# Attention stage of a fused attention, expert and feed-forward kernel: scatters, ranks and GpSimd's weight chunks get other steps

## The chip, the cores and the metric

The program runs on one core of one Trainium2 chip. The metric is the device time of one execution in microseconds; the kernel before and the changed kernel are timed in several runs each and compared by their medians. The engines are named as in the profile: PE is TensorE's matrix multiplication and PEld its weight load, DVE is VectorE, ACT is ScalarE, POOL is GpSimd and SP is SyncE, which here only issues transfers.

## The reference, cut to what matters

The inputs q and k are scaled by constant factors before the call. Three stages follow each other: attention with a window of 128, a mixture of 8 experts with the best two experts per token, and a feed-forward layer. Only the middle of the first two stages is touched by the change.

```python
# attention: batch 4, 8 heads, sequence 576, head size 64
scores = scale * np.matmul(q, k.transpose(0, 1, 3, 2))
mask = (rel >= 0) & (rel < window)                 # rel = query position - key position
scores = np.where(mask, scores + bias[None], -1000000000.0)
attn = np.exp(scores - scores.max(-1)); attn /= attn.sum(-1) + 1e-09
x = np.matmul(attn, v)                             # as 2304 tokens x 512
# experts
noisy_logits = x @ w_gate + np.log1p(np.exp(x @ w_noise)) * noise
top2 = np.argpartition(-noisy_logits, 2, axis=1)[:, :2]
top2_w = softmax of the two logits
for e in range(8):
    for k in range(2):
        mask = top2[:, k] == e
        h = np.maximum(x[mask] @ w1[e], 0.0)
        out[mask] += top2_w[mask, k, None] * (h @ w2[e])
# feed-forward
h = np.maximum(out @ w_in, 0.0)
return (h * h) @ w_out
```

## The kernel before, in words

**The attention loop.** The 2304 tokens are 18 tiles of 128 rows. A tile is worked in two halves of four heads, so there are 36 halves. One pass of the loop is a *step* v, and each step works on three halves at once: the scores of half v+2 (`s_step`), the transposes of half v+1 (`t_step`) and the product with the values and the norm of half v (`pv_step`, `norm`). In `s_step` PE writes the scores of four heads to a bank of PSUM with the tag "b", VectorE takes the bias and the row minimum in four instructions (L259, called minima below; each writes a column of a small tile `mx`), and ScalarE takes four exponentials. `t_step` transposes them on PE and copies them with ScalarE (L278). The tag "b" has two banks, which scores and products take by turns: the scores of one step can only start when the four minima of the step before have read theirs.

**The gate.** Two tiles form a *pair* p, from 0 to 8. When both tiles of a pair are done, the pair's gate follows over the next steps: `gate_t` transposes a tile (L330), `gate_w` and `gate_m` multiply, `gate_o` finds the two best experts (its first instruction, L360, multiplies two tiles in SBUF; L372 writes the one-hot tile `oh`), `rank` counts on PE how many tokens each expert has already (L384) and adds the pair to the running sum `acc` (L387), `place` turns ranks into slot numbers `pos` (its piece 0, L394, copies the ranks out of PSUM), and `scatter` writes token numbers to a table `slots` in memory by four indirect transfers of GpSimd (L425), each behind a small instruction on the tile `spacer`. The ranks, the transposes of `gate_t` and the other gate matmuls share one PSUM bank, with the tag "c", which has a single buffer: who comes next waits until the one before has been read.

**How the order is set.** The order of all engines is written out by hand. `at(v, slot, f, ...)` puts a piece of work into a table, and the loop calls `run(v, slot)` at fixed places of step v: slots 0 to 3 behind the four minima of VectorE, slot 4 after the transposes, slot 5 at the end. Each engine works through its own instructions in that order and waits only for data or buffers, so an engine with little to do, as GpSimd, may be ahead of the step that its instruction was written in. With o = 4p + 6 (for all pairs but the last), pair p's `gate_o` and `rank` are in step o, `place` is in step o+1 and the scatters are in steps o+1 and o+2. The steps with the same remainder by four therefore do the same kind of work. Steps 14 and 15, at 57.66 and 61.16 us, are o and o+1 of pair 2.

**Other work in the loop.** Every fourth step (v % 4 == 2) GpSimd converts one weight chunk for the first expert (`prep_one`): a cast (L108) and a subtraction of two SBUF operands (L110), 128x1024 each. `zero_rows` (step 4, slot 4) clears a tile and writes 128x3x512 zeros to `yg` in memory. When the first 6, 10 and 14 tiles have been scattered, SP reads a column of the table (`early_table`), GpSimd gathers those 128 token rows (`gather`) and PE transposes them into the first expert's input (`x_in`, L445). SP also issues every load of q, k, v and raw weights and every store of finished rows, in the order in which they are written.

Of the kernel before, what the change touches and what calls it, by code (L numbers as in the profile page):

```python
# [29 lines left out]
PARTS = (6, 10, 14)  # L30
# [19 lines left out]
def attn_moe_ffn(ctx: ExitStack, tc: tile.TileContext, qt, kt, vt, wgn, noise, w1, w2, w_in, w_out,  # L50
                 consts, out):
    nc = tc.nc
# [171 lines left out]
    def run(v, slot):  # L224
        for f, a in todo.pop((v, slot), []):
            f(*a)

    def s_step(v, now):
        if v >= NV:
            for n in range(4):  # L230
                run(now, n)
            return
        i, g = divmod(v, 2)
        if v == 1:
            warm_up(8)
        ps = bank("b")[:, :, 0:384].rearrange("p a (j n) -> p a j n", j=2)
        p2, mx = [], []
        for x in range(2):
            c = max(128 - 64 * ((2 * i + x) % TB), 0)
            if c:  # L240
                for a in range(2):
                    pa = slice(64 * a, 64 * a + 64)
                    nc.tensor.matmul(ps[64 * x:64 * x + 64, a, :, 0:c], ones[pa, 0:64],
                                     far[pa, 0:2 * c].rearrange("p (j n) -> p j n", j=2), start=True, stop=True)
        for j in range(2):
            p2.append(wk.tile([128, 2, 192], F32, name="p2", tag="p2", bufs=6))
            mx.append(wk.tile([128, 2], F32, name="mx", tag="mx", bufs=6))
            for x in range(2):
                b, t = divmod(2 * i + x, TB)
                k0 = max(64 * t - 128, 0)  # L250
                n = 64 * t + 64 - k0
                for a in range(2):
                    pa = slice(64 * a, 64 * a + 64)
                    nc.tensor.matmul(ps[64 * x:64 * x + 64, a, j, 192 - n:192],  # L254
                                     Q[i][pa, 2 * g + j, 64 * x:64 * x + 64], K[b][pa, 2 * g + j, k0:k0 + n],
                                     start=True, stop=True)
        for j in range(2):
            for a in range(2):
                nc.vector.tensor_tensor_reduce(  # L259
                    out=p2[j][:, a, :], in0=ps[:, a, j, :], in1=bias[:, 4 * g + 2 * j + a, :],  # L260
                    op0=OP.add, op1=OP.min, scale=-0.125, scalar=3.0e38, accum_out=mx[j][:, a:a + 1])
                run(now, 2 * j + a)
        for j in range(2):
            for a in range(2):
                nc.scalar.activation(out=p2[j][:, a, :], in_=p2[j][:, a, :], func=AF.Exp, bias=mx[j][:, a:a + 1],  # L265
                                     scale=-1.0)
        P2[v] = p2
# [151 lines left out]
            nc.vector.tensor_tensor(out=pos[:, two, :], in0=pf, in1=over, op=OP.min)  # L419
            del G["gs", p], G["oh", p], G["ri", p]  # L420

    def scatter(i):
        for k in range(2):
            nc.gpsimd.memset(spacer, 0.0)
            st = nc.gpsimd.indirect_dma_start(  # L425
                out=slots, out_offset=bass.IndirectOffsetOnAxis(ap=pos[:, i, k:k + 1], axis=0),
                in_=tok[:, i:i + 1], in_offset=None)
            for s in scatters:
                tc.declare_no_dep(st.ins, s.ins, reason="different rows")
            scatters.append(st)  # L430
# [81 lines left out]
    for p in range(NT // 2):  # L512
        v = 4 * p + 3
        end = v == last
        at(v - end, 4, gate_t, 2 * p)
        at(v + 1, 4, gate_t, 2 * p + 1)
        at(v + 2, 0 if end else 4, gate_w, p)
        at(v + 2, 0 if end else 5, gate_m, p)
        o = v + 2 if end else v + 3
        for n, c in enumerate((0, 0, 0, 1, 2)):  # L520
            at(o, c, gate_o, p, n)
        at(o, 4 if end else 5, rank, p)
        for n, c in enumerate((0, 1, 1, 2, 2, 3)):
            at(o + 1, c, place, p, n)
        at(o + 1, 3, scatter, 2 * p)
        if end or 2 * p + 2 == PARTS[-1]:
            at(o + 1, 4, scatter, 2 * p + 1)
        else:
            at(o + 2, 3, scatter, 2 * p + 1)
    at(0, 3, more_consts)  # L530
    at(4, 4, zero_rows)
    for j, (v, w, x) in enumerate(((17, 18, 20), (25, 26, 28), (2 * PARTS[-1] + 3, 2 * PARTS[-1] + 4, last + 1))):
        at(v, 4, early_table, j)
        at(w, 5, gather, 0, j, True)
        at(x, 5, x_in, 0, j)
    at(last, 5, keep_warm, 24)
    at(last + 2, 3, mm1_a, 0, 0)
# [12 lines left out]
    for v in range(-2, NV + 3):  # L550
# [4 lines left out]
        if 0 <= v < NV:  # L555
            i, g = divmod(v, 2)
            pv_step(v)
            for n in range(3):
                norm(i, g, n)
            if g:  # L560
                if nq < NT:
                    load_q(nq)
                    nq += 1
                while nv < 5 * B and v_free(nv - 5) <= 2 * i + 1:
                    load_v(nv)
                    nv += 1
                if nk < B and 2 * i + 1 >= 9 * (nk - 1) + 1:
                    load_k(nk)
                    nk += 1
            if v % 4 == 2 and nprep[0] < 8:  # L570
                prep_one("pool", "pool")
        run(v, 5)

# [737 lines left out]
```

## Time and profile before

| what | value |
|---|---|
| time, median of 3 runs | 983.34 us (981.25 to 984.23) |
| profiled execution: its time / its span | 981.14 us / 979.4 us |
| granted clock of PE, mean over the span | 0.998 |
| busy: PE / PEld / DVE / ACT / POOL | 959.1 / 879.9 / 670.4 / 464.2 / 418.5 us |
| PE busy from 0 to 150 us, the attention loop and its end | 139.2 us |
| transfers | 180.68 MB, 184 GB/s |

The span runs from the first to the last instruction of the profiled execution; 1.7 us of its time lie outside. The share of busy time is an average over stages, so the stage that is changed has to be read by itself: the attention loop ends at about 137 us, and the experts and the feed-forward layer fill the rest. In a row of a timeline the columns are the start in us, the duration in us, the engine, the line, the operation, what it writes and reads, how many instructions of the kind are merged, and in brackets the engine's idle time ahead of it with what ended it. Matmuls are pipelined: the time that a group of them takes on PE is read from its start to the start of the next group.

### The profile page before, as it was taken

The numbers are of one execution on the slowest core, as the hardware profiler recorded it, in microseconds if no ns is written. First come the engines' busy times: TensorE is split into PE (matmuls) and PEld (weight loads), VectorE is DVE, ScalarE is ACT, GpSimd is POOL, SyncE is SP. The second block draws the span as 40 slices with busy tenths as digits, with TensorE's granted clock in tenths as the row PEclk, the third lists the DMA queues.
The fourth block names the chain that finished last, engine by engine and source line by source line (L and its number), as shares of the span: only waits on it lengthen the run. The fifth ranks groups of instructions, "written<-read, shape, count | busy, mean of one in ns | idle before, by whom it ended". The sixth has DMA issues, their size and how long they took to land. (4 is left out here: it accounts for less than half of the span.)

```text
span 979.4 us, 19665 instructions
## 1 busy us (share of the span) xinstructions
PE 959.1 (98%) x7452; PEld 879.9 (90%) x7452; DVE 670.4 (68%) x1424; ACT 464.2 (47%) x887; POOL 418.5 (43%) x453
## 2 busy tenths in 40 slices
PE   8999999999999999999999999999999999999998
PEld 6676779898998989889898898999999998999998
DVE  4777764657676776757764436778576999877773
ACT  6776743434343343433343446655555564434331
POOL 1564543133242343414434032624211657988880
PEclk9999999999999999999999999999999999999999
DMA  9767624356668475756555453966637874443331
GB/s 333 263 216 265 210 88 152 111 169 220 211 204 258 151 231 196 243 189 194 204 199 200 147 171 95 299 195 173 166 97 229 233 217 149 148 142 130 130 108 44
DMA packets 118198, 180.68 MB, mean 184 GB/s; under 512 B 11104, under 2 KB 66032, under 8 KB 117712
## 3 DMA queue, kind: packets, MB, share of 16 engines
q1 hardware_dynamic: 107120, 147.46, 46.6%
q0 software_dynamic: 10976, 31.90, 10.7%
q8 instruction: 59, 0.97, 0.4%
q14 instruction: 43, 0.35, 0.1%
HBM read 125.02 MB, written 54.30 MB: 183 GB/s over the span
## 5 line engine op out<-in xcount | busy, mean ns | idle before, releaser
L869 POOL TENSOR_TENSOR gs<-xb 128x256 f32<-128x256 f32 x72 | 70.0, 992 | 29.1 <-DVE wc L869 12.6
L473 ACT ACTIVATE ha<-psa 128x384 fp32r<-128x384 f32 x64 | 31.3, 491 | 93.8 <-PE psa L469 92.3
L265 ACT ACTIVATE p<-p,mx 128x192 f32<-128x192 f32 x144 | 57.6, 450 | 29.5 <-DVE mx L259 28.6
L686 POOL TENSOR_TENSOR et<-ex,et 128x512 f32<-128x512 f32 x16 | 20.8, 1302 | 114.1 <-DVE ex L682 114.1
L474 DVE SCALAR_TENSOR_TENSOR ha<-psa,ha 128x384 fp32r<-128x384 f32 x64 | 35.4, 553 | 45.6 <-ACT ha L473 40.7
L707 POOL DMA_INDIRECT yr<-yg,pos x36 | 36.6, 1015 | 68.4 <-DVE ha L474 44.9
L259 DVE CUSTOM_DVE_ANT_0 p<-psb,bias 128x192 f32<-128x192 f32 x144 | 45.7, 351 | 14.7 <-PE psb L254 13.5
L425 POOL DMA_INDIRECT slots<-tok,pos x36 | 35.0, 972 | 45.9 <-DVE rs L311 33.6
L469 PE MATMUL psa<-xa,wa 128*128 128x384 f32 x288 | 53.4, 336 | 0.1
L469 PE MATMUL psa<-xa,wc 128*128 128x384 f32 x288 | 53.4, 336 | 0.0
L788 PE MATMUL psb<-wa,ha 128*128 128x512 f32 x216 | 52.8, 396 | 0.0
L438 POOL DMA_INDIRECT xr<-xd,gidx x40 | 43.3, 1084 | 21.9 <-issue 6.1
L792 ACT ACTIVATE yo<-psb 128x512 f32<-128x512 f32 x38 | 22.7, 598 | 59.2 <-PE psb L788 44.7
L469 PEld LDWEIGHTS psa<-xa,wa 128*128 128x128 f32 x288 | 49.5, 188 | 0.4 <-DVE ha L474 0.3
L469 PEld LDWEIGHTS psa<-xa,wc 128*128 128x128 f32 x288 | 49.6, 188 | 0.2
L869 DVE TENSOR_TENSOR wc<-gs,wc 128x512 fp32r<-128x512 f32 x48 | 48.5, 1049 | 0.0
L883 POOL DMA_DIRECT2D raw<-w x49 | 27.3, 562 | 47.6 <-DVE wb L869 20.2
L686 POOL TENSOR_TENSOR ex<-ex 128x512 f32<-128x512 f32 x12 | 15.6, 1302 | 74.0 <-DVE ex L682 74.0
L788 PEld LDWEIGHTS psb<-wa,ha 128*128 128x128 f32 x216 | 39.5, 188 | 7.8
L788 PE MATMUL psb<-wb,ha 128*128 128x512 f32 x176 | 46.3, 398 | 0.0
L110 DVE TENSOR_TENSOR wa<-raw,wa 128x1024 fp32r<-128x1024 f32 x20 | 25.9, 1293 | 27.8 <-ACT wa L106 27.8
L300 PEld LDWEIGHTS psb<-v,pt 64*64 64x64 f32 (+1 forms) x1056 | 32.6, 135 | 10.6 <-issue 7.9
(326 smaller groups left out, 2738.7 us busy)
## 6 DMA issues: line engine op xcount, KB each, us to landing
raw<-in_w_dram SPq DMA_DIRECT2D x64, 512.0 KB, 5.3
xb<-gmid SPq DMA_DIRECT2D x72, 256.0 KB, 2.9
v<-in_vt_dram SPq DMA_DIRECT2D x20, 520.0 KB, 6.0
yg<-yo SPq DMA_DIRECT2D x40, 256.0 KB, 3.0
raw<-w POOLq DMA_DIRECT2D x36, 256.0 KB, 3.7
gmid<-yo SPq DMA_DIRECT2D x48, 192.0 KB, 3.0
ex<-in_w_in_dram SPq DMA_DIRECT2D x16, 512.0 KB, 4.3
ex<-in_w_out_dram SPq DMA_DIRECT2D x16, 512.0 KB, 3.5
```

Of the source, the lines that this page charges most:

```text
L259: nc.vector.tensor_tensor_reduce(out=p2[j][:, a, :], in0=ps[:, a, j, :], in1=bias[:, 4 * g + 2 * j + a, :], op0=OP.add, op1=OP.min, scale= ...
L265: nc.scalar.activation(out=p2[j][:, a, :], in_=p2[j][:, a, :], func=AF.Exp, bias=mx[j][:, a:a + 1], scale=-1.0)
L300: nc.tensor.matmul(px[64 * x:64 * x + 64, a, j, :], l, r, start=not any(m[:2] == (x, a) for m in mms[:n]), stop=not any(m[:3] == (x, a, j) ...
L425: st = nc.gpsimd.indirect_dma_start(out=slots, out_offset=bass.IndirectOffsetOnAxis(ap=pos[:, i, k:k + 1], axis=0), in_=tok[:, i:i + 1], i ...
L438: nc.gpsimd.indirect_dma_start(out=XR[e, j], out_offset=None, in_=xd[0:PARTS[j] * 128] if early else xd, in_offset=bass.IndirectOffsetOnAx ...
L469: nc.tensor.matmul(o, w[wp][:, f * 128:(f + 1) * 128], x[:, xp, d, :], start=(n == 0), stop=(n == 11))
L473: nc.scalar.activation(out=hi, in_=ps, func=AF.Relu)
L474: nc.vector.scalar_tensor_tensor(out=lo, in0=ps, scalar=0.0, in1=hi.bitcast(F32), op0=OP.max, op1=OP.subtract)
L686: nc.gpsimd.tensor_tensor(out=x, in0=af, in1=cf, op=OP.add)
L707: nc.gpsimd.indirect_dma_start(out=YR[i, k], out_offset=None, in_=yg, in_offset=bass.IndirectOffsetOnAxis(ap=pos[:, i, k:k + 1], axis=0))
L788: nc.tensor.matmul(py, h[:, hq], wc[wp][:, wsl], start=(f + n == 0), stop=(f == 7 and n == 2))
L869: f(**a)
```

## The change

It has four parts. First, the ranks of pairs 0 to 5 move from slot 5 of step o to a new slot 6 of step o+1, which runs after the scores have been issued and ahead of the four minima; place moves with them, its six pieces now spread over steps o+1 (slots 1 and 3) and o+2 (slots 0, 1, 1 and 2). Second, the four scatters of these pairs go to slot 3 of steps o+2, o+3, o+4 and o+5, one to a step, and the small instruction ahead of each is no longer a memset but a copy of an element of `mx`, which the fourth minimum of the step writes. For the last three pairs the steps stay as they are, but for two scatters of pair 6, which go from slot 4 to slot 3 of the same step. Third, the early tables 0 and 1 are read at steps 19 and 27 instead of 17 and 25, gathered at slot 2 of steps 20 and 28 instead of slot 5 of 18 and 26, and transposed at steps 24 and 32 instead of 20 and 28. Fourth, `prep_one` of GpSimd runs in steps 4, 8, ..., 32 instead of 2, 6, ..., 30.

```diff
     def s_step(v, now):
         if v >= NV:
-            for n in range(4):
+            for n in (6, 0, 1, 2, 3):
                 run(now, n)
             return
...
+        run(now, 6)
         for j in range(2):
             for a in range(2):
                 nc.vector.tensor_tensor_reduce(
                     out=p2[j][:, a, :], in0=ps[:, a, j, :], in1=bias[:, 4 * g + 2 * j + a, :],
                     op0=OP.add, op1=OP.min, scale=-0.125, scalar=3.0e38, accum_out=mx[j][:, a:a + 1])
+                G["mx"] = mx[j]
                 run(now, 2 * j + a)
...
-    def scatter(i):
-        for k in range(2):
-            nc.gpsimd.memset(spacer, 0.0)
+    def scatter(i, *ks):
+        for k in ks:
+            nc.gpsimd.tensor_copy(spacer, G["mx"][0:1, 1:2])
             st = nc.gpsimd.indirect_dma_start(
...
-        at(o, 4 if end else 5, rank, p)
-        for n, c in enumerate((0, 1, 1, 2, 2, 3)):
-            at(o + 1, c, place, p, n)
-        at(o + 1, 3, scatter, 2 * p)
-        if end or 2 * p + 2 == PARTS[-1]:
-            at(o + 1, 4, scatter, 2 * p + 1)
-        else:
-            at(o + 2, 3, scatter, 2 * p + 1)
+        late_ = 2 * p + 2 < PARTS[-1]
+        q, per = (o + 2, 1) if late_ else (o + 1, 4 if end or 2 * p + 2 == PARTS[-1] else 2)
+        at(o + late_, 4 if end else 6 if late_ else 5, rank, p)
+        for n, c in enumerate((-3, -1, 0, 1, 1, 2) if late_ else (0, 1, 1, 2, 2, 3)):
+            at(q - (c < 0), c % 4, place, p, n)
+        for n in range(4):
+            at(q + n // per, 4 if end and n > 1 else 3, scatter, 2 * p + n // 2, n % 2)
     at(0, 3, more_consts)
     at(4, 4, zero_rows)
-    for j, (v, w, x) in enumerate(((17, 18, 20), (25, 26, 28), (2 * PARTS[-1] + 3, 2 * PARTS[-1] + 4, last + 1))):
+    for j, (v, w, x) in enumerate(((19, 20, 24), (27, 28, 32), (2 * PARTS[-1] + 3, 2 * PARTS[-1] + 4, last + 1))):
         at(v, 4, early_table, j)
-        at(w, 5, gather, 0, j, True)
+        at(w, 5 if j == 2 else 2, gather, 0, j, True)
         at(x, 5, x_in, 0, j)
...
-            if v % 4 == 2 and nprep[0] < 8:
+            if v % 4 == 0 and v and nprep[0] < 8:
                 prep_one("pool", "pool")
```

Three places show what moves. The lines of the changed kernel lie one or two further down than those of before (L384 becomes L386, L330 becomes L332, L394 becomes L396). Numbers behind a name, as in p_991, tell apart tiles of the same name.

GpSimd at the start of the program, before:

```order
L208 DMA slots<-zero 128x40
L108 CAST wa<-raw 128x1024
L110 ISA
L110 TENSOR_TENSOR wa<-raw,wa 128x1024
L507 MEMSET z 128x512
L508 DMA yg<-z 128x3x512
L108 CAST wa<-raw 128x1024
L110 TENSOR_TENSOR wa<-raw,wa 128x1024
```

The same place in the changed kernel:

```order
L208 DMA slots<-zero 128x40
L509 MEMSET z 128x512
L510 DMA yg<-z 128x3x512
L108 CAST wa<-raw 128x1024
L110 ISA
L110 TENSOR_TENSOR wa<-raw,wa 128x1024
L426 COPY spacer<-mx 1x1
L427 DMA slots<-tok,pos 9728x1
```

The write of the zero rows, which stood behind the first weight chunk, now stands ahead of it.

PE at the end of pair 1's rank, with the scores (L254), two groups of transposes (L276), the gate's transposes (L330) and the product with the values (L300) of step 11, before:

```order
L384 LDWEIGHTS ones
L384 MATMUL psc<-acc,ones 128x8
L384 LDWEIGHTS ones
L384 MATMUL psc<-acc,ones 128x8
L254 MATMUL psb<-k,q 64x192 x8
L276 MATMUL psa<-cst,p_912 128x128 x3
L276 MATMUL psa<-cst,p_918 128x128 x3
L330 MATMUL psc<-cst,xi 128x128 x4
L300 MATMUL psb<-v,pt 64x65 x14
```

The end of the same rank in the changed kernel:

```order
L386 LDWEIGHTS ones
L386 MATMUL psc<-acc,ones 128x8
L386 LDWEIGHTS ones
L386 MATMUL psc<-acc,ones 128x8
L278 MATMUL psa<-cst,p_908 128x128 x3
L278 MATMUL psa<-cst,p_914 128x128 x3
L332 MATMUL psc<-cst,xi 128x128 x4
L302 MATMUL psb<-v,pt 64x65 x14
```

The scores of the step now lie ahead of the rank, and the rank lies between them and the transposes; the gate's transposes, which write the same bank as the rank, follow in the same step as it.

VectorE in the same step (ISA rows are the minima, each followed by the row that writes its column of mx), before:

```order
L387 TENSOR_TENSOR acc<-acc,oh 128x16 x2
L259 ISA p_991,mx<-psb,bias 128x192
L259 ISA mx 128x1
L394 CAST ri<-psc 128x16
L259 ISA p_991,mx<-psb,bias 128x192
L259 ISA mx 128x1
L398 TENSOR_SCALAR ri<-ri 128x16
L399 SCALAR_TENSOR_TENSOR gs<-ri,cst 128x16
L407 SCALAR_TENSOR_TENSOR gs<-ri,gs 128x16
L409 TENSOR_SCALAR gs<-ri 128x16
```

And in the changed kernel:

```order
L389 TENSOR_TENSOR acc<-acc,oh 128x16 x2
L260 ISA p_972,mx<-psb,bias 128x192
L260 ISA mx 128x1
L260 ISA p_972,mx<-psb,bias 128x192
L260 ISA mx 128x1
L396 CAST ri<-psc 128x16
L260 ISA p_978,mx<-psb,bias 128x192
L260 ISA mx 128x1
L260 ISA p_978,mx<-psb,bias 128x192
L260 ISA mx 128x1
L400 TENSOR_SCALAR ri<-ri 128x16
L401 SCALAR_TENSOR_TENSOR gs<-ri,cst 128x16
```

The additions to acc stay ahead of the step's minima, although the rank that they wait for is now issued behind the scores; the copy of the ranks out of PSUM (CAST) moves from behind the first minimum to behind the second.

## Rows read from the trace of the kernel before

**Rows 1.** Busy time by engine, PE's granted clock and transfers in two stretches.

```profile
3.00:12.00 9.00, 7.34 (x77) 4.22 (x79) 2.40 (x16) 3.73 (x10) 0.00 (x0) 1.00 0.96 318
75.00:100.00 25.00, 23.14 (x377) 17.11 (x378) 16.77 (x105) 18.03 (x46) 12.07 (x19) 0.93 0.78 262
```

**Rows 2.** Waits of PE from 0 to 145 us: total, times, longest.

```profile
PE psc L384 <- DVE oh L372: 2.5, 5, 0.7
PE psb L254 <- DMA q<-in_qt_dram: 1.7, 1, 1.7
PE psa L445 <- DMA xr<-xd,gidx: 1.5, 1, 1.5
```

**Rows 3.** Timeline of PE, steps 15 and 16.

```profile
61.16 0.88 PE L254 MATMUL psb<-k,q 64*64 64x192 f32 x16
61.97 0.87 PE L276 MATMUL psa<-cst,p 128*128 128x128 f32 x6
62.69 0.63 PE L330 MATMUL psc<-cst,xi 128*128 128x128 f32 x4
63.25 1.13 PE L300 MATMUL psb<-v,pt 128*64 128x65 f32 x32
64.40 0.30 PE L243 MATMUL psb<-far,ones 64*64 64x256 bf16 x4
...
66.72 1.13 PE L300 MATMUL psb<-v,pt 128*64 128x65 f32 x32
67.67 0.28 PE L243 MATMUL psb<-far,ones 64*64 64x256 bf16 x4
```

**Rows 4.** L360 in steps o of pairs 0 to 6: length, its busy time.

```profile
29.76:33.53 3.77, 0.62 (x1) 1.00 0.90 297
...
117.10:120.39 3.29, 0.17 (x1) 1.00 0.60 211
sum 24.74, DVE 2.48; mean DVE 0.35
```

**Rows 5.** Timeline of GpSimd and VectorE in step 10.

```profile
43.12 2.36 POOL L110 TENSOR_TENSOR wa<-raw,wa 128x1024 fp32r<-128x1024 f32 x1
...
45.02 0.50 DVE L360 TENSOR_TENSOR gs<-gs,nz_sb 128x16 f32<-128x16 f32 x1
```

**Rows 6.** Timeline of VectorE, start of step 31.

```profile
120.91 0.36 DVE L387 TENSOR_TENSOR acc<-acc,oh 128x16 bf16<-128x16 bf16 x2
121.33 0.36 DVE L259 CUSTOM_DVE_ANT_0 p<-psb,bias 128x192 f32<-128x192 f32 x1
...
121.61 0.17 DVE L394 CAST ri<-psc 128x16 int32<-128x16 f32 x1
```

**Rows 7.** Timeline of PE behind the last scores.

```profile
131.86 0.63 PE L330 MATMUL psc<-cst,xi 128*128 128x128 f32 x4 [0.44 <-DVE gs L362]
...
133.48 0.21 PE L384 MATMUL psc<-oh,tri 128*128 128x8 bf16 x2
...
133.82 1.13 PE L300 MATMUL psb<-v,pt 128*64 128x65 f32 x32
```

**Rows 8.** Timeline of PE from the early transposes to the next product, twice.

```profile
83.13 0.66 PE L445 MATMUL psa<-cst,xr 128*128 128x128 f32 x4 [1.51 <-DMA xr<-xd,gidx]
...
87.47 1.13 PE L300 MATMUL psb<-v,pt 128*64 128x65 f32 x32
...
112.73 0.66 PE L445 MATMUL psa<-cst,xr 128*128 128x128 f32 x4
...
115.50 1.12 PE L300 MATMUL psb<-v,pt 128*64 128x65 f32 x28
```

**Rows 9.** Timeline of GpSimd: the zero rows.

```profile
26.75 0.80 POOL L508 DMA_DIRECT2D yg<-z  x1 [0.31 <-POOL z L507]
```

**Rows 10.** Timeline of GpSimd: pair 2's last scatter and the first gather.

```profile
68.56 0.97 POOL L425 DMA_INDIRECT slots<-tok,pos  x1 [0.23 <-issue]
...
76.35 1.00 POOL L438 DMA_INDIRECT xr<-xd,gidx  x1 [3.34 <-PE psa L276]
```

## The prediction

> **What bounds the kernel now.** The attention loop is read first by the timeline of PE: in step 15 scores, transposes, gate transposes and products follow each other at 61.16, 61.97, 62.69 and 63.25, and the next step starts at 64.40 [rows 3]. The reader is to see four groups that touch each other, with 0.81, 0.72, 0.56 and 1.15 us from start to start; the last is 0.95 where nothing holds the next scores (66.72 to 67.67 [rows 3]), so VectorE, whose minima free the bank, holds PE here for 0.2 us. The list of PE's waits then names what else it stands for: 2.5 us for the one-hot tile ahead of the ranks, 1.7 us for q at the start, 1.5 us for the first early gather [rows 2]. Everything that the change can win on PE's path lies in these waits and in what hangs on them. A microsecond on PE in this loop is a microsecond of the whole, since PE works without a pause into the experts' stage.
>
> **Steps o, where gate_o and rank stood.** The seven steps o of pairs 0 to 6 take 24.74 us together, from 3.77 to 3.29, and L360 in them takes from 0.62 to 0.17 [rows 4]. The cause is in the timeline of step 10: GpSimd's subtraction runs from 43.12 to 45.48, and L360, which starts at 45.02, ends at 45.52 [rows 5]. It was held until GpSimd had done. VectorE's chain of four minima and the gate is what the next scores wait for, so a hold lengthens the step by its length. Pair 6, whose L360 took 0.17 us, shows a step without a hold: 3.29 us. The changed chunks come after the scatter of a step o+2 that now waits for that step's fourth minimum, some 3 us into it; two instructions of about 1 us and the subtraction of 2.36 us end about 8 us after that step's start, and the next L360 comes 1.3 us into the second step after it: 7.9 us with two steps of 3.27 us (64.40 to 67.67 [rows 3]), and more, since the step between carries two further gate products. So the hold goes, by little. The rank leaves the step, but the scores wait for the fourth minimum in any case; I give nothing for that. Pairs 0 to 5 take 24.74 - 3.29 = 21.45 us now and 6 x 3.29 = 19.74 then: **-1.7 us**. If a chunk comes 0.4 us later than I think, some of it stays; the bounds are -1.7 and 0.
>
> The Trainium skill, page SBUF — State Buffer, section "Who interferes with whom", says that a VectorE instruction with two SBUF inputs and a GpSimd instruction that reads SBUF exclude each other for the whole length of the first. The rows agree to 0.04 us. By the rule the cast would hold L360 as well, which no row here shows; if it did, it would change the sum only in the steps behind a gather, below.
>
> **Steps o+1, where the rank goes.** Count from the start of the scores. They take 0.81, and the rank 0.34 (133.48 to 133.82 [rows 7]), so the transposes start at 1.15 and end at 1.87. The last rank matmul ends some 0.06 us after the rank's slot, at about 1.2; with a signal to VectorE, the additions to acc start at 1.27 and hold the first minimum for 0.42 (120.91 to 121.33 [rows 6]). First minimum 1.69, second 1.97, and at 2.25 the copy of the ranks out of the bank, which takes 0.17 (spacing and length again from [rows 6]): 2.42, and 0.06 for the signal. The gate's transposes need that bank and can start at 2.48, where PE was ready at 1.87: a new wait of 0.6 us in each of six steps. That such a wait happens is seen behind the last scores: there L330 stood 0.44 us for L362, the last reader of the bank [rows 7]. Before, the copy was due 0.3 us ahead of the transposes and cost nothing. The step then takes 2.48 + 0.56 + 0.95 = 3.99, where step 15 took 3.24 to 3.3 [rows 3], 0.7 more: **+4.2 us** for six. What is queued behind the waiting transposes on PE is the product with the values, its norm and the next scores. Without the wait the step would still carry the rank: 0.81 + 0.34 + 0.72 + 0.56 + 0.95 = 3.38, or +0.1 each, +0.7 in all. These are the bounds; I take the upper one, because the order of the instructions leaves no way around it. The later exponentials of that step push later copies on ScalarE; no row shows PE waiting for them in these steps, so I take nothing, with 0.1 us a pair as the dear end.
>
> The pieces of place in step o+2 lengthen VectorE's chain there by about 1.1 us, to some 3.2, as long as PE's own work in it (64.40 to 67.67 [rows 3]): nothing, or 0.1 us each.
>
> **The first early gather.** PE stood 1.5 us for it [rows 2], and right after this wait the granted clock fell: 0.93 as the mean from 75 to 100 us [rows 1], which is half speed for some 3.5 us, the 1.2 of 2.4 GHz. From L445 to the next product but one it took 83.13 to 87.47, 4.34 us, and 112.73 to 115.50, 2.77, for the same groups at full clock [rows 8]: 1.57. Four steps later the rows have long arrived: the gather comes about 11 us after the start of step 19 by the time from scatter to gather, 7.8 us [rows 10], and `x_in` at the end of step 24 lies about 21 us after it. **-3.1 us**; the dear end is -1.5, if the clock falls elsewhere.
>
> **The zero rows.** In the changed order GpSimd issues the 128x3x512 zeros, 786 KB, behind nothing that waits, so at about 3 us instead of 26.75 [rows 9]. Then the transfer engines are 0.96 busy and move 318 GB/s [rows 1], and the third scores already stand 1.7 us for q [rows 2]. At that rate 786 KB are 2.4 us. The cheap end is 0, if q comes first. I take **+2.0**, near the dear end, since the write is issued before q's load is served. Then PE's wait for q is 3.7 us, and nothing later gives it back, as PE fills the steps that follow.
>
> The Trainium skill, page DMA: Bandwidth & Descriptors, section "Queues, rings and completion order", says that each transfer engine serves the queues that have work by turns. By it the zeros would take every second turn, be done before q, and cost the whole 2.4; the sum would be 0.4 us higher. The trace of before has no two full queues at the start.
>
> **Chunks behind the two gathers.** GpSimd takes its instructions in order, so the gather in steps 20 and 28, which waits for the table, holds the scatter and the chunk behind it. With the table 7.8 us behind the last scatter [rows 10] the subtraction comes some 5 us later than in other periods and falls into steps 22 and 23 (30 and 31), among L360, L372 and the additions to acc, all with two SBUF operands. A hold is between 0 and 2.36 us [rows 5]; I take 1.0 each: **+2.0 us**. The minima themselves wait for the copy only if it is three steps late; it is not.
>
> **Other parts at nothing.** Copies instead of memsets on `spacer` are 0.1 us on an engine with time. The k load of the fourth batch now stands behind the table read of step 19, with about 1 us to spare at step 24.
>
> **The sum.** -1.7 + 4.2 - 3.1 + 2.0 + 2.0 = +3.4 us on the profiled 981.14 us (span 979.4), so 984.5 for an execution like that. It lay 2.2 us under the median; on 983.34 the forecast is 986.7 us, 0.35% slower. About 0.3%, 2.95 us, is what a measurement of this kernel can tell from no change.
>
> **Rivals.**
> - No new wait at the gate's transposes, and so no slowdown. It decides at one point: whether the copy of the ranks is done when the transposes end at 1.87. For it: 0.3 us of room before. Against it: the additions stand ahead of both minima. 3.4 - 4.2 + 0.7 = -0.1: 983.2 us. Chance 0.2.
> - The zeros wait for a gap and cost nothing: +1.4, 984.7 us. The queues at 0.96 speak against it. 0.15.
> - The longer wait for q lets the clock fall as at 83 us: another 1.6 us [rows 8], 988.3 us. PE stood 1.7 us there without it. 0.15.
> - The change does not do what it says, and chunks still meet L360: +1.7 more, 988.4 us. 0.08.
> - My forecast, with what is around it: 0.42, from 985 to 988.5.
>
> Faster by over 0.3% needs the first two at once and no holds behind the gathers (3.4 - 3.5 - 2.0 - 2.0 = -4.1): with some of the first rival's and second rival's chance 0.1. Slower by over 0.3%: the likely half of the forecast, the third and the fourth: 0.5. Within: 0.4. The range of 8 in 10 goes from just under the first rival to beyond the clock case: 982.5 to 990.
>
> **What the next profile would show.** L330's successor, L332, in six steps with about 0.6 us of idle time ended by VectorE's copy; steps o at 3.3 and steps o+1 at 4.0; L360's successor at 0.17 in all pairs but those behind gathers; no wait of L445's successor for xr and no low clock near 83 us; the third scores waiting over 3 us for q. The prediction is wrong if the steps o+1 stay at 3.3 to 3.4, or if the third scores start at 11.7 as before.

## The result and the profile after

The changed kernel takes 992.17 us (median of 4 runs, 991.68 to 993.71) beside 982.3 us (980.02 to 984.23) for the kernel before on the same chip: ratio 1.0111, interval 1.0089 to 1.0133. The forecast was 986.7 us with a range of 982.5 to 990.0, so the direction was right and the time lies 2.2 us beyond the range. The profiled execution took 991.87 us, span 989.7, which is 10.3 us above the span of before.

The kernel before takes 980 to 982 us on the chip of this comparison and on that of one later experiment, and 1005 to 1011 us on the four chips of the other experiments; one of these four was used three times and gave 1005 us each time. The former are called chips of the first kind, and the forecast is about them; the second kind has a part of its own below, since a number measured there can't be laid beside one of the first kind.

The first view is again the list of PE's waits, now of the changed kernel, 0 to 150 us: total, times, longest.

```profile
PE psb L254 <- DVE rs L313: 4.3, 4, 2.2
PE psb L254 <- DMA q<-in_qt_dram: 3.6, 2, 2.4
PE psc L332 <- DVE ri L396: 2.9, 6, 0.6
PE psc L332 <- DVE gs L364: 2.4, 1, 2.4
PE psc L386 <- DVE oh L374: 1.7, 1, 1.7
```

Against [rows 2], the wait for xr is gone, and that for the one-hot tile stands once instead of five times. The third row is the forecast's new wait: six times, about 0.5 us. The second is the longer wait for q, as long as forecast. Of the first, its longest wait of 2.2 us was looked for, and so was the last, both smaller; the fourth was not looked for at all.

To see what each is worth, take from PE's timeline the first score matmul (L254) of every step and subtract. This table is worked out so; both kernels are in profiled executions on the first kind.

| stretch | before, us | after, us | difference | forecast |
|---|---|---|---|---|
| start, to the fifth step's scores | 16.60 | 19.94 | +3.3 | +2.0 |
| steps o, pairs 0 to 3 and 5 | 18.16 | 16.74 | -1.4 | -1.7 |
| steps o+1, pairs 0 to 5 | 19.76 | 23.20 | +3.4 | +4.2 |
| the two steps at the first early gather | 10.86 | 6.99 | -3.9 | -3.1 |
| steps o of pairs 4 and 6, behind the gathers | 6.58 | 9.80 | +3.2 | +2.0 |
| other steps, to the last scores | 54.95 | 55.88 | +0.9 | 0 |
| last scores to the experts' first matmul | 13.26 | 15.92 | +2.7 | 0 |
| from there to the end of the span | 839.23 | 841.23 | +2.0 | 0 |

Three places carry what the forecast lacks. First the start, in PE's timeline of the changed kernel, and the busy row of 13 to 20 us, whose last three numbers are the granted clock, the share of the transfer engines and GB/s.

```profile
9.66 0.67 PE L254 MATMUL psb<-k,q 64*64 64x64 f32 x16 [1.19 <-DMA q<-in_qt_dram]
13.54 0.88 PE L254 MATMUL psb<-k,q 64*64 64x192 f32 x16 [2.41 <-DMA q<-in_qt_dram]
15.47 1.65 PE L302 MATMUL psb<-v,pt 128*64 128x65 f32 x17
...
13.00:20.00 7.00, 6.46 (x85) 5.08 (x88) 3.46 (x22) 3.49 (x10) 0.00 (x0) 0.76 1.04 381
```

PE waits twice for q, 3.6 us together where the forecast had 3.7; then the clock falls to half from about 14.8 to 18.2 us, and that is the other part of the loss. Second, pair 4's step o, behind the first gather: timelines of SyncE, GpSimd, VectorE and PE.

```profile
85.64 0.33 SPq L500 DMA_DIRECT2D gidx<-slots  x1
...
88.18 0.99 POOL L440 DMA_INDIRECT xr<-xd,gidx  x1 [4.72 <-DVE mx L260]
...
91.65 2.34 POOL L110 TENSOR_TENSOR wb<-raw,wb 128x1024 fp32r<-128x1024 f32 x1
...
90.95 0.65 DVE L362 TENSOR_TENSOR gs<-gs,nz_sb 128x16 f32<-128x16 f32 x1
...
92.81 1.23 DVE L374 TENSOR_TENSOR oh<-iota,sel 128x32 bf16<-128x32 uint32 x1
...
94.56 0.88 PE L254 MATMUL psb<-k,q 64*64 64x192 f32 x16 [2.20 <-DVE rs L313]
```

GpSimd stands 4.7 us ahead of the gather. The row names a minimum, but SP issues the read of the table (L500) only at 85.64, so it is the table that the gather waits for. The chunk behind the gather comes late, L362 takes 0.65 us instead of 0.17, and the one-hot (0.19 us where nothing holds it) ends at 94.04, 0.05 us after the subtraction. The next scores wait 2.2 us for VectorE, the longest of the first row of the waits. Third, the last gate but one, and what comes after it.

```profile
135.58 1.05 POOL L108 CAST wb<-raw 128x1024 fp32r<-128x1024 f32 x1
136.71 2.33 POOL L110 TENSOR_TENSOR wt<-raw,wb 128x1024 fp32r<-128x1024 f32 x1
...
137.00 2.08 DVE L362 TENSOR_TENSOR gs<-gs,nz_sb 128x16 f32<-128x16 f32 x1 [0.23 <-ACT gs L356]
...
139.50 0.63 PE L332 MATMUL psc<-cst,xi 128*128 128x128 f32 x4 [2.38 <-DVE gs L364]
...
141.48 1.83 PE L302 MATMUL psb<-v,pt 128*64 128x65 f32 x32
```

The eighth chunk, due two steps later and queued behind seven scatters of the last pairs, holds the gate's first product to its own end (139.04 and 139.08). PE waits 2.38 us, where it waited 0.44 [rows 7], and then runs at half clock: the products take 1.83 us, not 1.13. Nothing ties the last row of the table to the change: in the twenty profiles of this study, of whatever version, this stretch takes 839.2 to 847.3 us, and in the four of one and the same version (the repaired change, below) 843.7 to 847.3.

### The profile page after: what moved, and what is told of

It is laid out like the page before. It is cut to its first block, busy times and chain, and to the rows that moved or that the text cites. A ratio compares the mean times of both kernels' runs of the same rounds, so it can differ in the third digit from the quotient of the medians.

```text
span 989.7 us, 19679 instructions
## 1 busy us (share of the span) xinstructions
PE 958.9 (97%) x7452; PEld 880.6 (89%) x7452; DVE 676.6 (68%) x1424; ACT 463.9 (47%) x887; POOL 423.5 (43%) x453
## 5 line engine op out<-in xcount | busy, mean ns | idle before, releaser
L260 DVE CUSTOM_DVE_ANT_0 p<-psb,bias 128x192 f32<-128x192 f32 x144 | 46.1, 351 | 16.7 <-PE psb L254 13.6
L440 POOL DMA_INDIRECT xr<-xd,gidx x40 | 44.7, 1117 | 26.0 <-DVE mx L260 9.4
```

What stands on the lines that cost most here:

```text
L260: nc.vector.tensor_tensor_reduce(out=p2[j][:, a, :], in0=ps[:, a, j, :], in1=bias[:, 4 * g + 2 * j + a, :], op0=OP.add, op1=OP.min, scale= ...
L440: nc.gpsimd.indirect_dma_start(out=XR[e, j], out_offset=None, in_=xd[0:PARTS[j] * 128] if early else xd, in_offset=bass.IndirectOffsetOnAx ...
```

## The experiments

**The change's terms one by one.** Four kernels on a chip of the second kind. In the first, one line moves the zero rows behind the chunk:

```
-    at(4, 4, zero_rows)
+    at(4, 5, zero_rows)
```

> The changed kernel with the zero rows' memset and transfer put behind GpSimd's first weight chunk, as they stood before. Theory (the start's loss is the zero rows' transfer beside the first loads, both the 1.8 us of waits for q and the 1.6 us of half clock that follows it): the second and third scores start near 8.7 and 11.7 us, no half clock before 20 us, scores of step 4 near 16.6 instead of 19.94; whole time 3.3 us below the changed kernel, about 988.9. Rival 1 (the half clock has another cause): the waits go, 1.6 us stay, 990.4. Rival 2 (the zero rows are not what q waits for): nothing moves, 992.

1002.88 us, ratio to the kernel before 0.9985 (0.9962 to 1.0008). The second scores start at 8.53 us, so their wait for q is gone; the third still wait 3.0 us, and the clock still falls: fifth scores at 20.41. One profile tells little here; the twenty of this study tell more, though across versions and chips. With the zero rows early (six profiles) the fifth scores start at 19.57 to 20.84 us, mean 20.2, and the clock falls in each. With them late (fourteen) seven start at 16.6 to 16.9 without a fall and seven at 18.8 to 20.4 with one; mean 18.0. So the zero rows cost 2.2 us on the mean: 1.0 by the wait (third scores at 13.3 instead of 12.3 us) and 1.2 behind it, where the clock is at half. The pair that was compared shows 3.3 because the kernel before had drawn the better start.

```
-        late_ = 2 * p + 2 < PARTS[-1]
+        late_ = False
```

> The changed kernel with the ranks, their placing and the number of scatters for each step put back where they stood before the change for all pairs; the copy that binds the scatters, the gathers, x_in and the chunks stay as changed. Theory (the late copy of the ranks holds PSUM's single buffer from the gate transposes): steps o+1 fall from 3.75-4.0 to 3.3 us, no wait of PE for the copy of the ranks, whole time about 3.4 us below the changed kernel (988.8), less what four scatters close together on GpSimd cost by moving the chunks (0 to 2). Rival (the longer steps o+1 come from GpSimd's bound scatters): they stay at 3.8 to 4.0 and the time at 992.

The steps o+1 that no other wait disturbs take 3.27 to 3.38 us, against 3.98 to 4.76 in the changed kernel on such a chip: the theory on the place. The whole time doesn't follow, 1.0011 (0.9983 to 1.0039). One reason is told under the second kind; another is that the steps o of pairs 4 and 6 take 7.09 and 7.37 us here, against 6.00 and 6.08 in the changed kernel on such a chip.

```
-        at(w, 5 if j == 2 else 2, gather, 0, j, True)
+        at(w, 5, gather, 0, j, True)
```

> The changed kernel with the first two gathers behind the weight chunk of their step on GpSimd. Theory (a gather that waits for its table pushes the chunk's subtraction onto VectorE's gate operations): the steps o of pairs 4 and 6 fall from 4.95 and 4.85 to about 3.4 us, the gate's first product and the one-hot there to 0.17 and 0.2 us, whole time 3.1 us below the changed kernel, about 989. Rival (the gather's own descriptors hold VectorE): these two steps stay above 4.4 and the time above 991.

The steps o of pairs 4 and 6 take 4.00 and 3.88 us, against 6.00 and 6.08 of the changed kernel on a chip of this kind, the one-hot 0.19 us; L362 is still held to 0.77 and 0.65 us. That is 4.2 us less, so the gather's place makes most of the hold. The whole time can't tell it from nothing: ratio 0.9982 (0.9961 to 1.0003).

```
-    ... ((17, 18, 20), (25, 26, 28), ...
+    ... ((17, 18, 24), (25, 26, 32), ...
```

> The kernel before with one edit: the splits of the first two gathers stand at steps 24 and 32 instead of 20 and 28, tables and gathers where they were. Theory (the 1.5 us wait for the gathered rows and the half clock behind it are the only cost of the early place): the steps of 5.50 and 5.36 us near 83 and 89 us fall to 3.2-3.8, no half clock there, whole time 3.1 to 3.9 us below the kernel before (0.9960 to 0.9968). Rival (the split itself of 0.6 us and a new collision at steps 24 and 32 give it back): less than 1.5 us.

This edit is made to the kernel before. 0.9999 (0.9971 to 1.0026): nothing, for a reason that its profile shows and that led to the next runs.

**The second kind of chip.**

> The changed kernel once more, as it is, beside the kernel before on the chip of this call, so that the others of the call have it beside them. The first comparison gave 1.0111 [1.0089, 1.0133] at 982 us for the kernel before; the four runs above were on a chip where the kernel before takes 1005 us and TensorE shows idle between matmuls that wait for nothing. Theory (the change's costs are the same on every chip): ratio near 1.010. Rival (on such a chip those gaps fall into waits that the change adds, and hide them): ratio below 1.004.

Ratio 1.0004 (0.9977 to 1.0030): on this kind the change costs nothing that can be told. Its waits are all there and even longer: the six for the copy of the ranks are 6.2 us together instead of 2.9. In five of the six the additions to acc start 0.95 to 1.01 us behind the start of the last rank matmul, on the first kind 0.20.

> The kernel before, one look, for its rows on a chip of the kind of the runs above (1005 us, where the change shows no difference). Theory (there TensorE's own instructions come late in the attention, and a wait gives them time to catch up, so that the waits that the change adds cost nothing): PE shows over 6 us of idle that waits for nothing before 150 us, where the first trace of this kernel shows none, and the changed kernel less than half of that (2.7 us). Rival (the chip is slower for transfers, and the waits for data grow): the idle stands before waits for loads, under 2 us of it waits for nothing. If the chip is of the first kind, rows as in the first trace.

PE's waits and its timeline, kernel before, second kind (the step whose scores start at 39.97 on the first kind):

```profile
PE psb L254 <- issue: 5.1, 10, 1.1
PE psb L300 <- issue: 3.8, 10, 0.4
PE psa L445 <- issue: 1.2, 2, 0.9
PE psb L243 <- issue: 0.8, 2, 0.4
...
42.69 0.42 PE L254 MATMUL psb<-k,q 64*64 64x128 f32 x3 [0.38 <-issue]
43.42 0.55 PE L254 MATMUL psb<-k,q 64*64 64x128 f32 x3 [0.31 <-issue]
44.17 0.32 PE L254 MATMUL psb<-k,q 64*64 64x192 f32 x1 [0.19 <-issue]
44.87 0.69 PE L254 MATMUL psb<-k,q 64*64 64x192 f32 x9 [0.39 <-issue]
```

"Issue" is idle time in which PE waits for nothing that the profile shows. It is 10.9 us before 150 us, where the first trace of the same kernel has none, and it comes as small groups of matmuls some 0.7 us apart; the steps in which it falls take 4.5 to 6.4 us instead of 3.2 to 3.8. The last scores start at 143.9 instead of 126.9 us. In the changed kernel on this kind:

```profile
PE psb L302 <- issue: 2.4, 3, 1.1
PE psb L254 <- issue: 0.3, 2, 0.2
```

2.7 us. Where the gaps went is seen by the place of the steps. In the kernel before all of them stand in steps o+2 and o+3, none in steps o and o+1. This table adds the steps 6 to 29, from scores to scores, in us.

| profile | six steps o+1 | six steps o+2 and six o+3 |
|---|---|---|
| first kind, before | 19.8 | 46.1 |
| first kind, after | 23.2 | 42.8 |
| second kind, before | 19.8 | 61.3 |
| second kind, after | 28.2 | 45.9 |
| second kind, all nine profiles with the ranks late | 26.0 to 28.3 | 44.7 to 46.4 |
| second kind, all seven with the ranks as before | 19.8 to 21.6 | 52.1 to 67.1 |

Two pairs of versions differ only in where the ranks, their placing and the scatters stand: the changed kernel and the one with the ranks put back above, and the two repaired ones below. In them the late ranks lengthen the six steps o+1 by 6.6 and 5.0 us together and shorten the twelve steps behind them by 6.2 and 10.4. That a wait lets late instructions catch up fits this, and is not shown. What the change costs elsewhere stays: in these two profiles the last scores start 5.5 us later than in the kernel before (149.3 us), as on the first kind (5.6), and the span is 2.1 us longer. The medians of the whole are equal all the same, 1004.9 and 1005.2 us.

> The changed kernel with the copy of the ranks from PSUM one VectorE score operation earlier (behind the first, not the second) in steps o+1 of the first six pairs. Theory (that copy is what PE's gate transposes wait for, 0.5 us in six steps): the wait falls by the 0.28 us of one score operation, to about 0.2 us, and steps o+1 from 3.75-4.0 to 3.5-3.7; whole time 1.6 us below the changed kernel (ratio to it 0.9984). Rival (the copy only waits longer for the ranks and the transposes start as before, the step being set by something else): no change in steps o+1.

```
-        for n, c in enumerate((-3, -1, 0, 1, 1, 2) if late_ else ...
+        for n, c in enumerate((-4, -1, 0, 1, 1, 2) if late_ else ...
```

Steps o+1 of pairs 0 to 5 are shorter by 0.27, 0.29, 0.31, 0.29, 0.28 and 0.28 us than in the changed kernel beside it: what they wait for is this copy, to the length of one score operation. Whole time 0.9997 (0.9976 to 1.0018).

> The changed kernel with GpSimd's eighth weight chunk, step 32, made by ScalarE (copy) and VectorE (subtraction) instead. Theory (in the last steps of the attention GpSimd's late subtraction holds the gate's first product of pair 7, 2.08 us, PE waits 2.4 us for it and then runs 3.4 us at half clock): that product takes 0.2 us, PE's wait before the gate's transposes falls below 0.6 us, no half clock near 141 us; from the scores of step 35 to the first matmul of the experts 13.3 us instead of 15.9, whole time 2.6 us below the changed kernel, less up to 1 us for the two operations moved. Rival (the tail is late for the third gather's table, not for the chunk): 15.9 us stay, whole time unchanged.

```
-                prep_one("pool", "pool")
+                prep_one(*(("pool", "pool") if v < 32 else ("act", "dve")))
```

1.0015 (0.9987 to 1.0042), and no test: on this chip the gate of the changed kernel itself came clear of the chunk (L362 0.18 us, PE's wait 0.40).

> The changed kernel with four repairs together: zero rows behind the first chunk, the first two gathers behind their step's chunk, the copy of the ranks one score operation earlier, the eighth chunk on ScalarE and VectorE. Theory (the terms add: 3.3 + 3.2 + 1.6 + 2.6 by the first chip's rows): 10.7 us below the changed kernel on a chip of the first kind, which makes it equal to the kernel before (ratio 0.999). On a chip of the second kind, where single repairs gave 0.9985, 0.9982, 0.9997 and 1.0015 against 1.0004 of the change: 0.997. Rival (the repairs overlap, each only uncovers the next wait): no better than the best one, 0.998 there.

0.9963 (0.9941 to 0.9986), as the sum of the single repairs had it for this kind; the interval also holds the rival's 0.998, and no single repair's whole time was told from the kernel before's. Three repeats follow.

> The same with the ranks, their placing and the scatters for each step as before the change, in place of the earlier copy: of the change there remain the later splits of the gathered rows, the bound scatters and the later chunks. Theory: on a chip of the first kind 3.3 + 3.2 + 3.4 + 2.6 below the changed kernel, 2.6 us faster than the kernel before (0.9974). On a chip of the second kind the missing waits bring TensorE's late instructions back: 1.000, not better than the run with the ranks late. Rival: the order of the chips' kinds doesn't matter, and it is the fastest on either (0.997).

1.0012 (0.9985 to 1.0038). The two differ only in where the ranks, their placing and the scatters stand: late ranks, which cost 3.4 us in the steps o+1 on the first kind, are worth 4.4 us of the whole here. The theory's reason shows only in part: PE's idle for nothing before 150 us is no longer here, 4.3 us against 4.5, but the steps behind the ranks are, as the table above has it, and the granted clock from the fifth to the last scores is 0.93 instead of 0.96.

> The kernel before with the splits of the first two gathers at steps 24 and 32, once more. Theory: on a chip of the first kind 3.1 to 3.9 us faster than the kernel before (0.9960 to 0.9968), the fastest of all; on one of the second kind 0.9999 as measured there, since the freed time is taken by TensorE's late instructions. Rival: 1.000 on either kind.

1.0011 (0.9981 to 1.0042). The steps of 6.37 and 3.80 us at the first gather became 4.54 and 6.68: the stall went, and in the next step PE stood for nothing shown (0.6 us) and ran at half clock.

> The changed kernel with its four repairs once more. On a chip of the first kind (the kernel before near 982 us): the terms add, 992.2 less 10.7 = 981.5, ratio 0.999; scores of step 4 at 16.6 us, steps o of pairs 4 and 6 near 3.4, steps o+1 near 3.6, wait for the last gate's first product under 0.6 us, no half clock in the attention. On one of the second kind (1005 us): 0.9963 as measured, within 0.002. Rival: the first value there was chance, 0.999 or more.

Second kind again, 0.9965 (0.9941 to 0.9990).

**The chunks alone, on the first kind.**

```
-            if v % 4 == 0 and v and nprep[0] < 8:
+            if v % 4 == 2 and nprep[0] < 8:
```

> The changed kernel with GpSimd's weight chunks, and with them the zero rows behind the first, at the steps where they stood before; ranks, scatters, gathers and splits as changed. Theory (start, holds behind gathers and the last gate all come from the moved chunks): the steps o of pairs 4 and 6 back to 3.4-3.6 us, scores of step 4 not later than in the kernel before on this chip, GpSimd's chunks done before the last gate; steps o+1 stay long. On a chip of the first kind 992.2 - 3.3 - 3.1 - 2.7 + up to 1.7 of holds in steps o = 983 to 985; on one of the second kind 0.9965, like the four repairs. Rival (the chunks now meet the gate's or the ranks' operations in other steps, as before): 0.999 to 1.001.

The kernel before took 980.4 us on this chip, this one 1002.81: ratio 1.0204 (1.0165 to 1.0243). Both theories fall for the whole, as no one had it slower than the change; two of the three places hold. The steps o of pairs 4 and 6 take 3.40 us each, and from the last scores to the experts' first matmul it is 13.29 us, as before the change: holds and tail come from the moved chunks. The start did not come back in this profile: one wait of 3.5 us for q, half clock behind it, fifth scores at 19.40. And steps o+1 of pairs 1 to 5 take 5.09 to 5.50 us. PE's waits, and the timelines of the three engines in pair 1's step o+1:

```profile
PE psc L332 <- DVE ri L396: 9.5, 6, 1.8
...
51.61 1.66 DVE L389 TENSOR_TENSOR acc<-acc,oh 128x16 bf16<-128x16 bf16 x2 [0.66 <-PE psc L386]
51.99 1.04 POOL L108 CAST wa<-raw 128x1024 fp32r<-128x1024 f32 x1
53.12 2.38 POOL L110 TENSOR_TENSOR wa<-raw,wa 128x1024 fp32r<-128x1024 f32 x1
54.38 1.15 DVE L400 TENSOR_SCALAR ri<-ri 128x16 int32<-128x16 int32 x1
...
54.06 0.63 PE L332 MATMUL psc<-cst,xi 128*128 128x128 f32 x4 [1.77 <-DVE ri L396]
```

With the ranks late and the chunks where they were, the additions to acc meet GpSimd's cast, 1.66 us instead of 0.37, and PE's wait for the copy behind them grows from 0.48 to 1.77 us. The later ranks need the later chunks. In the sum of this kernel, five such steps are 7.0 us above the changed kernel; a further 3.2 us of PE's idle waits for nothing shown, once, at 135 us, with half clock behind it. The clock also falls at 85.9 and 120.0 us, each time behind such a wait of L332, 1.8 us, and the stretch behind the attention is 4.4 us longer, which is within what it varies by.

> The kernel before without the second half of the P times V matmuls (the part for the middle 128 keys' rows of every tile but a batch's first), so that TensorE has 16 matmuls and their weight loads less in most steps. Theory (on a chip of the second kind TensorE's instructions come too slowly for the attention's small matmuls, some 0.7 us for a handful): with a quarter fewer of them the idle that waits for nothing before 150 us falls from 10.9 to under 3 us, and the scores of step 35 start near 112 us, beyond the 19 us of matmul time left out (143.9 - 19 = 125). Rival (the gaps stand at fixed places of the program or of time, whatever the number of instructions): over 7 us of such idle, and 125 or later.

This ran on a chip of the first kind, and its profile has no such gaps, so it says nothing about them. It says something else, about the attention loop alone: what it leaves out changes the output and with it the experts' work. The edit to the kernel before is

```
-                        elif a == 0 or t > 1:
+                        elif a == 0 and t == 0:
```

and 480 of 1056 matmuls of that line go, 13.1 us of PE's busy time (16.6 to 3.5 us in their 64x64 form). Still the last scores start at 123.93 us, only 3 us earlier, and PE waits 7.2 us for the one-hot tile, where it waited 2.5 [rows 2]. The clock is at half for 3.4 us more as well. The whole took 984.93 us in its one run, beside 980.4 for the kernel before.

> The changed kernel with its four repairs. On a chip of the first kind the terms read from the first comparison add: start 3.3, holds 3.1, copy of the ranks 1.6, last gate 2.6; 10.6 below the changed kernel, 981 to 982 where the kernel before takes 980 to 982, ratio 0.997 to 1.002; steps o of pairs 4 and 6 3.4 us instead of 4.9, steps o+1 3.5 to 3.7, wait for the last gate's first product under 0.6 us. Rival (the repairs uncover other waits, as undoing the chunks did): 1.006 or more. On one of the second kind 0.9964 as twice before.

> As for the repairs in the call before: on a chip of the first kind ratio 0.997 to 1.002 (theory: the terms add) or 1.006 and more (rival: they uncover other waits); on one of the second kind 0.993 to 0.9965 as three times before.

Both fell on the second kind: 0.9930 (0.9896 to 0.9963) and 0.9898 (0.9854 to 0.9943). That leaves out the rival's 0.998. On these two chips it is the kernel before that is slower, 1010 and 1011 us; the repaired change takes 1001 to 1003 us on all of its chips, and each time it is the fastest version beside it. Its gather repair is not whole: the steps o of pairs 4 and 6 still take 3.7 to 5.0 us.

> The kernel before with the splits of the first two gathers at steps 24 and 32. On a chip of the first kind: the steps of 5.50 and 5.36 us at 78 to 89 us fall to 3.3 to 3.9, no half clock there; 3.1 to 3.9 us faster than the kernel before, 0.9960 to 0.9968. Rival (the freed time brings a GpSimd chunk onto the gate's or ranks' operations, which then costs as much): 0.999 to 1.002. On one of the second kind 1.000 as twice before.

> As for the later splits alone in the call before: on a chip of the first kind 0.9960 to 0.9968 (theory: the stall and the half clock behind it go, nothing comes back) or 0.999 to 1.002 (rival: the freed time goes to a collision with GpSimd's chunks); on one of the second kind 1.000 to 1.002 as three times before.

1.0016 (0.9982 to 1.0050) and 1.0000 (0.9968 to 1.0031): the later splits alone are worth nothing on the second kind, four times. Neither these splits nor the repaired change have been timed on a chip of the first kind, so whether the four repairs give back the 10 us there stays open.

## Why the prediction was right in part and wrong in the sum

- **Steps o: right**, -1.4 for -1.7; in every pair clear of a gather the gate's first product is free of GpSimd's subtraction, and these steps take 3.2 to 3.4 us.
- **Steps o+1: right**, place, cause and size: six waits of L332 for the copy, steps of 3.75 to 4.0 us, +3.4 for +4.2. The one-operation shift and the ranks put back both show it, on the second kind of chip.
- **The first early gather: right**, -3.9 for -3.1 on the first kind. There it rests on the two profiles; the later splits alone have run on the second kind only.
- **The zero rows: right in the wait, near in the sum by luck.** In the pair compared the wait for q is 3.6 us (3.7 forecast) and the loss 3.3, as in the rival with the falling clock. Over all profiles the loss is 2.2 us, but the wait makes 1.0 of it and the half clock, which the sum left out, 1.2. Among the starts with late zero rows the clock falls behind waits of 1.9 to 3.5 us and doesn't behind waits of 1.4 to 2.5; why stays open.
- **Chunks behind the gathers: right in place, too small.** "A hold is between 0 and 2.36 us; I take 1.0 each": it was 1.6 each, since the subtraction meets both the gate's first product and the one-hot.
- **What failed is the step that put every other part at nothing**, the eighth chunk above all: +2.7 us in the tail. Of the 6.9 us between the 10.3 of the two spans and the forecast's 3.4, 5.6 stand in the three rows of the table that have a 0 (2.7, 2.0 and 0.9); the start and the chunks behind the gathers were too small by 2.5, and the other three terms came out 1.3 lower than forecast. The prediction's list of parts at nothing does not name the eighth chunk. I moved the chunks by two steps and followed the two behind the gathers, but not the last one, which comes into the gate of pair 7 with seven scatters ahead of it. PE's wait there was in my own rows [rows 7], as 0.44 us with no hold; a hold of one subtraction makes it 2.4, and the clock falls. That the place of the chunks makes this is shown by the run that undid it (13.29 us, as before), in one profile; the run made for the eighth chunk alone could not test it.
- **The +2.0 behind the attention** lies within what the same code varies by, and nothing ties it to the change. Of the +0.9 in other steps, 0.5 us is one wait of L351 for `gt` in pair 4's step o+3; the rest stays open.
- **"A microsecond on PE in this loop is a microsecond of the whole"** fits the waits added on the first kind. It does not hold for PE's own work, of which 13 us less gave 3, nor on the second kind, where the steps behind the late ranks' waits are shorter by as much as the waits, or more.

## What to carry to other kernels

When a periodic piece of work on a side engine moves by some steps, follow every instance, the last above all: the end of a loop is where its neighbours change and where nothing behind it gives the time back. Two edits that seem apart may need each other; undo one at a time before calling either good or bad. And compare a change of one per cent on more than one chip, since a wait may cost nothing where the engine would have stood anyway.

## What the hardware showed unexpectedly

- PE's idle time that waits for nothing, 10.9 us on chips of the second kind and none in the first trace of the same code. All five profiles there of the kernel before and of its later splits alone have them in steps o+2 and o+3 only. In the first 150 us the instruction queue moved 16 packets of 16 KB there and 16 to 18 on the first kind, at about the same share of the transfer engines (0.7 and 0.8%). That these gaps are instructions coming late fits that steps behind a long wait have fewer of them, but was not shown; the kernel meant to test it ran on the other kind. The Trainium skill, page Runtime: NRT & Kernel Launch, section "Instruction fetch mechanics", has the sequencer fetch blocks of 16 KB by itself, with the cost mostly hidden; the packets agree in size, and whether it is hidden here no run tells.
- GpSimd's cast with one input holds a VectorE sum of two SBUF tensors as its subtraction does (1.66 us for two additions of 0.37 together), and the subtraction holds an integer tensor_scalar with a single SBUF tensor too (L400: 1.15 us instead of 0.17, ending 0.03 us after it). The Trainium skill, page SBUF — State Buffer, section "Who interferes with whom", names both: the sum through its second input, the tensor_scalar as an operation that can enter a mode that takes both ports. The score operation, which reads PSUM and one SBUF tensor, stayed at 0.35 us beside the same subtraction.
